# Gate and value products of the first network's last batch by one level of Strassen's method, with the down products laid between them

## The chip, the cores and the metric

One core of a Trainium2 chip runs the whole program. The metric is device time in microseconds (us) from start to end of one execution; lower is better. The engines are named as the profile names them: PE multiplies matrices (PEld is its weight load), DVE works element by element, ACT applies functions and copies, SP issues all DMA transfers of this kernel, in one queue and in order; POOL does almost nothing here. PE writes to eight PSUM banks of 512 fp32 words in each partition, from which DVE or ACT must take the results.

## What is computed

Attention over 4 batches of 512 local tokens (a window of 32 on either side, and 32 global tokens for each batch), then two feed-forward networks on all 4·(512+32) = 2176 rows. The change lies in the first network.

```python
a_l = sm(concat([scale * q_l @ k_g.T, where(|i-j| <= 32, scale * q_l @ k_l.T, -1e9)]))
x = concat([sm(scale * q_g @ k_all.T) @ v_all, a_l @ v_all])   # 2176 rows of 512
# first network: 512 -> 1536 -> 512
g = x @ w_gate;  y = (g * sigmoid(g) * (x @ w_val)) @ w_out
# second network: 512 -> 2048 -> 512
h = y @ w_in;    out = (max(h, 0) + alpha * min(h, 0)) @ w_out2
```

## The kernel before

**Precision.** Each fp32 operand is split into a high and a low part (`hi` by an ACT copy that rounds to fp32r, `lo` by a DVE subtraction). A product is three matmuls, hi·hi, hi·lo and lo·hi (`passes`). The weights arrive as 64-bit floats; `convert` makes them fp32 with two passes of ACT and three of DVE over 1024 words per partition.

**Order of work.** Hidden features come in 12 blocks f of 128, in two halves GA (0 to 5) and GB (6 to 11). Activations lie with features on the partitions and tokens on the columns.

1. Attention of batch 0, then the first network for batches 0, 1 and 2 (512 columns each, two visits of six blocks per batch, `visit1`). In a visit each block has a gate product (12 matmuls of 512 columns into bank `g`, `mm12`), an ACT Silu, a value product (bank `v`), a DVE multiplication and the split of `h`; the down product of the block before (12 matmuls) is added up in banks `acc0` to `acc3`. The attention of the next batch, the conversion of weights, and `w2_prepare` (see below) are laid between the blocks by a `pump`.
2. Batch 3 and the 128 global rows, 640 columns, in four visits: columns 0 to 255 and 256 to 639, each for GB and for GA, with the same products in pieces of 256 or 384 columns (L856 for gate and value, L894 for down). After the second visit of each range the sums lie in `y3` and `yg`.
3. The second network, on three chunks of 768, 768 and 640 columns and eight pairs j of hidden blocks. Its first product already uses Strassen's method in Winograd's form (`up`: seven products of 6 matmuls, L1216, where plain blocks need eight; DVE adds at L1224 and L1254; an ACT copy at L1247), its second is plain (`down`, L1284).

**Weights of the second network.** `w2_prepare` is a generator: for each of 16 matrices it loads 1 MB of 64-bit words, converts it, forms Strassen's four sums (L838), splits, and stores high and low parts in DRAM, from where `fetch` loads them later. The pump takes a step of it when nothing else is to be converted; what is left is taken during batch 3.

**What sets the order.** Everything up to `nc.flush()` (all of step 1) is recorded, and `Planner` lays it out by a list schedule: each operation has a price by its engine and size, PE's order of recording gives target times, and an operation on another engine is due `SLACK` = 60 us after its target, or sooner if PE needs it. Behind the flush, the framework's own scheduler orders the code nearly as written. On each engine instructions are taken in order.

**Room.** Weights of the first network lie in six 1 MB slots for gate and value (`wgv`) and three for down (`wo`). The operands of the matmuls of a batch, high and low, lie in `xa` (4 × 640 columns each).

## Time and profile before

| | |
|---|---|
| three runs | 896.65 us median, 895.0 to 897.09 |
| profiled execution: its time, its span | 896.52 us, 894.7 us |
| PE busy | 875.3 us, 98% of the span |
| PEld, DVE, ACT busy | 761.3, 607.6, 501.2 us |
| granted PE clock, mean | 0.996 |
| moved by DMA | 217.25 MB, 243 GB/s |

The span runs from the first to the last instruction; what lies around it is 1.8 us. A busy engine counts from the start to the modelled end of each instruction. The profile gives shares for the whole program; the stages differ, so the views below are taken by stage.

### The profile page before, as it was taken

What the parts mean: (1) busy time and instruction counts of PE and PEld (TensorE: products, weight loads), DVE (VectorE), ACT (ScalarE), POOL (GpSimd) and SP (SyncE); (2) the same over time, 40 slices, a digit from 0 to 9 for tenths busy, and PEclk for the clock granted to TensorE, in tenths of its full rate; (3) what the DMA queues carried; (4) which work ended last, traced back from release to release, by engine and by line L of the source; (5) the groups of instructions that cost most, each with busy time, mean ns of one, the idle gap of its engine ahead of it and who ended that gap; (6) DMA issues with size and microseconds to landing.
All of it is one profiled execution on the core that took longest, in us unless ns stands there. A gap on an engine that the chain in (4) does not pass through costs nothing.

```text
span 894.7 us, 17087 instructions
## 1 busy us (share of the span) xinstructions
PE 875.3 (98%) x6940; PEld 761.3 (85%) x6940; DVE 607.6 (68%) x1261; ACT 501.2 (56%) x1007; POOL 0.7 (0%) x6
## 2 busy tenths in 40 slices
PE   5899999999999999999999999999999999999997
PEld 4677778788788787889999999999999999989896
DVE  3898889856377465567411257777896777977776
ACT  5889999767586584555312125434555434554442
POOL 0000000000000000000000000000000000000000
PEclk9899999999999999999999999999999999999999
DMA  9799988688957568744463255646375554675631
GB/s 345 267 410 412 363 327 338 263 325 306 375 191 279 224 243 323 282 182 148 167 225 127 95 180 203 228 159 262 145 265 229 209 215 174 250 275 222 279 141 59
DMA packets 34030, 217.25 MB, mean 243 GB/s; under 512 B 4000, under 2 KB 4640, under 8 KB 10272
## 3 DMA queue, kind: packets, MB, share of 16 engines
q1 hardware_dynamic: 33952, 216.17, 63.5%
q8 instruction: 54, 0.88, 0.4%
q14 instruction: 24, 0.20, 0.1%
HBM read 167.66 MB, written 48.50 MB: 242 GB/s over the span
## 4 chain that ended last, share of the span: by engine, by line
PE 60%; DVE 0%; issue 0%
PE ps_acc L1284 21%; PE ps_a L1216 8%; PE ps_v L1216 5%; PE ps_g L1216 5%; PE ps_acc L894 5%; PE ps_v L856 5%; PE ps_g L856 5%; PE acc L270 2%; PE v L270 2%; PE g L270 2%; PE a L270 0%; DVE dbl L270 0%; DVE oacc L1289 0%; DVE h L270 0%
## 5 line engine op out<-in xcount | busy, mean ns | idle before, releaser
L1284 PE MATMUL ps_acc<-w,hring 128*128 128x512 f32 x816 | 194.1, 391 | 0.0
L1284 PEld LDWEIGHTS ps_acc<-w,hring 128*128 128x128 f32 x816 | 152.1, 188 | 29.8
L270 PE MATMUL g<-xa,w 128*128 128x512 f32 x432 | 107.7, 398 | 1.8 <-ACT sg L270 1.0
L270 PE MATMUL v<-xa,w 128*128 128x512 f32 x432 | 107.1, 396 | 0.0
L270 PE MATMUL acc<-h,w 128*128 128x512 f32 x432 | 106.4, 395 | 0.6 <-DVE h L270 0.5
L1233 ACT ACTIVATE r<-c 128x384 f32<-128x384 f32 (+1 forms) x96 | 47.9, 499 | 95.8 <-DVE c L1224 95.8
L270 PEld LDWEIGHTS g<-xa,w 128*128 128x128 f32 x432 | 79.0, 188 | 21.4 <-issue 1.8
L1289 DVE TENSOR_TENSOR oacc<-ps_acc,oacc 128x512 f32<-128x512 f32 x119 | 81.8, 690 | 22.3 <-PE ps_acc L1284 21.1
L270 PEld LDWEIGHTS acc<-h,w 128*128 128x128 f32 x432 | 79.8, 188 | 19.7 <-DVE h L270 1.6
L270 PEld LDWEIGHTS v<-xa,w 128*128 128x128 f32 x432 | 79.3, 188 | 18.3 <-issue 1.4
L1238 ACT ACTIVATE hring<-g 128x384 fp32r<-128x384 f32 (+1 forms) x96 | 48.6, 506 | 54.7 <-DVE g L1235 54.2
L270 ACT ACTIVATE e<-e,mx 128x128 f32<-128x128 f32 (+1 forms) x136 | 57.1, 422 | 17.6 <-DVE mx L270 17.4
L1239 DVE TENSOR_TENSOR hring<-g,hring 128x384 fp32r<-128x384 f32 (+1 forms) x96 | 51.1, 532 | 19.4 <-ACT hring L1238 16.4
L1235 DVE SCALAR_TENSOR_TENSOR g<-g,nal,r 128x384 f32<-128x384 f32 (+1 forms) x96 | 56.7, 590 | 10.2 <-ACT g L1234 9.6
L270 ACT ACT_TABLE_LOAD x40 | 51.3, 1283 | 7.7 <-PE g L270 6.4
L1234 ACT ACTIVATE g<-c 128x384 f32<-128x384 f32 (+1 forms) x96 | 47.9, 499 | 13.4 <-DVE hring L1239 13.4
L1216 PE MATMUL ps_a<-w 128*128 128x384 f32 (+1 forms) x288 | 51.4, 326 | 0.0
L920 DVE TENSOR_TENSOR t<-ps_v,sg 128x384 f32<-128x384 f32 (+1 forms) x18 | 10.8, 601 | 55.4 <-PE ps_v L856 51.9
L1216 PEld LDWEIGHTS ps_a<-w 128*128 128x128 f32 x288 | 47.9, 188 | 0.3 <-DVE c L1224 0.3
L856 PE MATMUL ps_v<-xa,w 128*128 128x256 f32 (+1 forms) x288 | 45.1, 308 | 0.0
L856 PE MATMUL ps_g<-xa,w 128*128 128x256 f32 (+1 forms) x288 | 45.1, 308 | 0.0
L270 DVE TENSOR_TENSOR t<-v,sg 128x512 f32<-128x512 f32 x36 | 24.7, 687 | 30.0 <-ACT sg L270 12.1
(184 smaller groups left out, 1354.6 us busy)
## 6 DMA issues: line engine op xcount, KB each, us to landing
dbl<-in_w_dram SPq DMA_DIRECT2D x28, 1024.0 KB, 6.1
w<-w2sx SPq DMA_DIRECT2D x24, 1024.0 KB, 4.8
w<-w2ss SPq DMA_DIRECT2D x24, 1024.0 KB, 6.3
w<-w2so SPq DMA_DIRECT2D x24, 1024.0 KB, 5.4
v<-in_v_dram SPq DMA_DIRECT2D x15, 1024.0 KB, 9.6
qk<-in_qk_dram SPq DMA_DIRECT2D x14, 688.0 KB, 9.3
w2sx<-dbl SPq DMA_DIRECT2D x8, 1024.0 KB, 6.5
w2ss<-dbl SPq DMA_DIRECT2D x8, 1024.0 KB, 5.0
```

Source lines behind the costliest of these rows:

```text
L270: last[o.eng] = getattr(getattr(self.nc, o.eng), o.op)(*o.args, **o.kw)
L856: nc.tensor.matmul(out=o, lhsT=a, rhs=x, start=(i == 0), stop=(i == 11))
L894: mm = nc.tensor.matmul(out=acc[m][:, 0:n], lhsT=a, rhs=x, start=(first and not second), stop=(f == fs[-1] and j == 2 and (second or not h ...
L920: nc.vector.tensor_tensor(out=t[:, 0:nn], in0=v[:, 0:nn], in1=sg[:, 0:nn], op=ALU.mult)
L1216: nc.tensor.matmul(out=o[:, 0:n], lhsT=left(name, a, k), rhs=x[:, b, k, 0:n], start=(i == 0), stop=(i == 5),)
L1233: nc.scalar.activation(out=rr, in_=u, func=ACTF.Relu)
L1234: nc.scalar.activation(out=g, in_=u, func=ACTF.Relu, scale=-1.0)
L1235: nc.vector.scalar_tensor_tensor(out=g, in0=g, scalar=nal[:, i:i + 1], in1=rr, op0=ALU.mult, op1=ALU.add)
L1238: nc.scalar.activation(out=hi, in_=g, func=ACTF.Copy)
L1239: nc.vector.tensor_tensor(out=lo, in0=g, in1=hi, op=ALU.subtract)
L1284: nc.tensor.matmul(out=o, lhsT=a, rhs=x, start=(i == 0), stop=(i == 5))
L1289: nc.vector.tensor_tensor(out=oacc[tb], in0=o, in1=oacc[tb], op=ALU.add)
```

## The change

Batch 3 and the global rows (640 columns) go through the first network in six pairs j of blocks, f = 2j and 2j+1, and no longer in four visits. For each pair, gate and value are each made by `winograd`, now a function that both networks share: columns in two halves of `N3` = 320, input features in two halves of 256, hidden features in two halves of 128; seven products (`NAMES`) of 6 matmuls of 320 columns. They use two banks, `g` and `v`, in turn (`bank3`), since `a0` and `a1` now hold down sums: the eight accumulators of `down3` are the 640 columns of four output blocks, 384 columns in each of `acc0` to `acc3` and 256 in halves of `a0` and `a1`. The down product of pair j-1 is cut into 16 pieces of 3 matmuls, of which one or two follow each product of pair j from the third on.

Strassen needs four sums of each pair's weights (`w1ss`). `w1_sums` makes them from the split weights while these lie in their slots for batch 1: for each pair, for gate and value, two DVE adds of 512 columns for each block (high plus low), four of 256 in `block_sums`, an ACT copy, a DVE subtraction of 1024, and two stores. In batch 3, `fill` loads 4 MB for each pair (weights and sums, gate and value), the next pair's gate slots as soon as this pair's gate products are through. `third` makes the operands (sums of columns, splits) at the end of batch 2. The global rows are kept whole in `yg`, and split there.

`w2_prepare` has finer steps (`convert_steps`, `split_store`), halves its DVE passes behind the flush (`cuts`), and stores from the buffers it worked in; the pump takes 1.7 of its steps at a time and at most 98 before the flush; the rest follow the products of batch 3, one step after each. The planner's due times are capped at 10 us before the end of PE's work. The code of the second network is the same, but for shared functions and the order of sums in a tile.

```diff
+N3 = 320
+NAMES = ("b11", "t2", "t3", "t1", "b21", "t4", "b22")
...
-            d = target[i] + (0.0 if eng[i] == "tensor" else self.SLACK)
+            d = target[i] if eng[i] == "tensor" else min(target[i] + self.SLACK, at - self.LAST)
...
+    def w1_sums(f):
+
+        j = f // 2
+        for i, z in enumerate("gv"):
+            w = wt[(1, f, z)].bitcast(F32)
+            if f % 2 == 0:
+                sums1[z] = ex.tile([128, 1024], F32, tag="y3%d" % i)
+            s = sums1[z]
+            nc.vector.tensor_tensor(
+                out=s[:, 512 * (f % 2):512 * (f % 2) + 512], in0=w[:, 0], in1=w[:, 1], op=ALU.add
+            )
+            if f % 2 == 0:
+                continue
+            for _ in block_sums(s, s):
+                pass
+            w1ss[j, z] = dram.tile([128, 2, 1024], F32, name="w1ss%d%s" % (j, z))
+            hi = xa.rearrange("p h k c -> p (h k) c")[:, :, S:640]
...
+    def split_store(dst, hi, lo):
+
+        nc.scalar.activation(out=hi, in_=lo, func=ACTF.Copy)
+        for a, b in cuts(lo.shape[1]):
+            yield
+            nc.vector.tensor_tensor(out=lo[:, a:b].bitcast(F32R), in0=lo[:, a:b], in1=hi[:, a:b], op=ALU.subtract)
+        nc.sync.dma_start(out=dst[:, 0], in_=hi.bitcast(F32))
+        nc.sync.dma_start(out=dst[:, 1], in_=lo)
...
-        visit1(1, 0, 512, GB, False, p, after_f=reload(GA, GB))
-        visit1(1, 0, 512, GA, True, p, boundary=lambda: xprep(2))
+        visit1(1, GB, False, p, after_f=summing(reload(GA, GB)))
+        visit1(1, GA, True, p, after_f=summing(lambda f, ps: None), boundary=lambda: xprep(2))
...
-        visit1(3, 0, 256, GB, False, p, third=late)
-        visit1(3, 256, 640, GB, False, p, after_f=reload(GA, GB), third=late)
-        visit1(3, 0, 256, GA, True, p, third=late)
-        for _ in w2gen:
-            pass
...
+            for name in NAMES:
+                o = banks()
+                product(o, name)
+                if name == "b11":
+                    s["p1"] = alp.tile([128, NT], F32, tag="p1", name="p1")
+                    nc.scalar.activation(out=s["p1"][:, 0:n], in_=o[:, 0:n], func=ACTF.Copy)
+                elif name == "t2":
+                    s["u2"] = add("u2", o, s["p1"])
+                elif name == "t3":
+                    s["u3"] = add("u3", o, s["u2"])
+                elif name == "t1":
+                    c22 = add("c", o, s["u3"])
+                    u2 = s["u2"]
+                    nc.vector.tensor_tensor(out=u2[:, 0:n], in0=o[:, 0:n], in1=u2[:, 0:n], op=ALU.add)
+                    use(1, 1, c22[:, 0:n])
...
+                yield
...
-        visit1(3, 256, 640, GA, True, p, after_f=more, boundary=last_ops, third=late)
...
+            def gate(f, q, c):
+                nc.scalar.activation(out=sg[f][:, q], in_=c, func=ACTF.Silu)
+
+            def value(f, q, c):
+                t = work.tile([128, 512], F32, tag="t", name="t")[:, 0:N3]
+                hi, lo = (h[:, f, p, N3 * q:N3 * q + N3] for p in range(2))
+                nc.vector.tensor_tensor(out=t, in0=c, in1=sg[f][:, q], op=ALU.mult)
+                nc.scalar.activation(out=hi, in_=t, func=ACTF.Copy)
+                nc.vector.tensor_tensor(out=lo, in0=t, in1=hi, op=ALU.subtract)
...
+                for _ in winograd(N3, ops1, left, bank3, use):
+                    n += 1
+                    if n > 2:
+                        for _ in range(1 if n % 3 else 2):
+                            next(todo, None)
+                    if j or n > 4:
+                        next(w2gen, None)
+                if z == "g":
+                    again(j, z)
+            for _ in todo:
+                pass
+            again(j, "v")
+            todo = down3(j)
```

Three places show how instructions move. First PE, from the last matmuls of batch 2 on; before, the gate (`ps_g`) and value (`ps_v`) products of three pairs of blocks stand first, 24 matmuls of 256 columns to a bank:

```order
L270 MATMUL acc_126<-h_152,w_145 128x512 x3
L856 MATMUL ps_g<-xa,w_133 128x256 x12
L856 MATMUL ps_g<-xa,w_134 128x256 x12
L856 MATMUL ps_v<-xa,w_133 128x256 x12
L856 MATMUL ps_v<-xa,w_134 128x256 x12
```

and now (`w_137`, `w_138`, `xa`, `hring_4298` hold the operands, `w_133` to `w_136` the weights and sums of pair 0):

```order
L272 MATMUL acc_126<-h_152,w_145 128x512 x3
L1214 MATMUL ps_v<-w_137,w_133 128x320 x6
L1214 MATMUL ps_g<-w_138,w_134 128x320 x6
L1214 MATMUL ps_v<-xa,w_134 128x320 x6
L1214 MATMUL ps_g<-xa,w_134 128x320 x6
L1214 MATMUL ps_v<-xa,w_133 128x320 x6
L1214 MATMUL ps_g<-xa,w_133 128x320 x6
L1214 MATMUL ps_v<-hring_4298,w_134 128x320 x6
```

Seven gate products, then seven value products stand one behind another in two banks; pair 0 has no down pieces between them, and the first such piece (L1271) stands behind the fourteenth.

Second DVE at the same place; before, from the last `h` of batch 2 on (`yp_95` takes batch 2's sums, `raw` and `dbl` are `w2_prepare`):

```order
L270 TENSOR_TENSOR h_152<-t_150,h_152 128x512
L740 TENSOR_SCALAR raw<-raw 128x1024
L270 TENSOR_TENSOR yp_95<-acc_121,yp_95 128x2x256
L270 TENSOR_TENSOR yp_95<-acc_122,yp_95 128x2x256
L270 TENSOR_TENSOR yp_95<-acc_125,yp_95 128x2x256
L270 TENSOR_TENSOR yp_95<-acc_126,yp_95 128x2x256
L741 SCALAR_TENSOR_TENSOR dbl<-dbl 128x1024
L744 SCALAR_TENSOR_TENSOR raw<-raw,dbl 128x1024
```

and now, from the last of these four sums on (four sums of columns into `e_115` and `e_116` stand ahead of them, behind the last `h`):

```order
L272 TENSOR_TENSOR yp_95<-acc_126,yp_95 128x2x256
L272 TENSOR_TENSOR xa<-e_115,xa 128x640
L272 TENSOR_TENSOR xa<-e_116,xa 128x640
L760 TENSOR_SCALAR raw<-raw 128x1024
L769 SCALAR_TENSOR_TENSOR raw<-raw,dbl_112 128x512
L1001 TENSOR_TENSOR hring_4298<-y_166,hring_4298 128x2x256
L1001 TENSOR_TENSOR hring_4298<-yg,hring_4298 128x2x64
L1222 TENSOR_TENSOR u_4333<-ps_g,p_4324 128x320
L769 SCALAR_TENSOR_TENSOR raw<-raw,dbl_112 128x512
L1222 TENSOR_TENSOR u_4342<-ps_v,u_4333 128x320
L760 TENSOR_SCALAR raw<-raw 128x1024
L1222 TENSOR_TENSOR c<-ps_g,u_4342 128x320
```

The adds that empty PE's two banks (L1222) now stand behind the splits of operands and between passes of `w2_prepare` (L760, L769).

Third DVE in batch 1, between a value product's `t` and the next softmax; before:

```order
L270 TENSOR_TENSOR t_150<-v_129,sg_148 128x512
L270 TENSOR_TENSOR dbl_111<-raw_131,dbl_111 128x2x512
L270 TENSOR_TENSOR h_151<-t_150,h_151 128x512
L270 TENSOR_SCALAR o_130<-a_113,rc_128 128x64 x2
```

and now:

```order
L272 TENSOR_TENSOR h_151<-t_150,h_151 128x512
L272 TENSOR_TENSOR y_139<-y_139,xa 128x1024
L272 TENSOR_TENSOR raw_131<-raw_131,dbl_111 128x1024
L272 TENSOR_TENSOR o_130<-a_113,rc_127 128x512
L272 TENSOR_TENSOR y_166<-w_134 128x512
L272 TENSOR_TENSOR y_166<-w_133 128x512
L272 TENSOR_TENSOR y_166<-y_166 128x256 x4
```

The rows with `y_139` and `y_166` are `w1_sums`: they stand among the rows that PE waits for.

## Rows read from the trace of the kernel before

**Rows 1.** The page: busy time of each engine, granted PE clock in 40 slices.

```profile
PE 875.3 (98%) x6940; PEld 761.3 (85%) x6940; DVE 607.6 (68%) x1261; ACT 501.2 (56%) x1007; POOL 0.7 (0%) x6
PEclk9899999999999999999999999999999999999999
```

**Rows 2.** Stretches by stage: busy us of each engine, clock, DMA share, GB/s.

```profile
0.00:172.00 172.00, 157.86 (x2089) 124.39 (x2090) 136.85 (x349) 151.22 (x311) 0.70 (x6) 0.98 0.88 340
172.00:300.00 128.00, 127.50 (x1198) 102.00 (x1197) 80.07 (x184) 88.17 (x164) 0.00 (x0) 1.00 0.77 291
300.00:410.00 110.00, 109.85 (x970) 88.88 (x969) 64.39 (x135) 64.94 (x120) 0.00 (x0) 1.00 0.66 249
410.00:537.00 127.00, 127.00 (x867) 127.00 (x866) 47.80 (x82) 33.68 (x63) 0.00 (x0) 1.00 0.43 157
537.00:895.00 358.00, 353.12 (x1824) 319.07 (x1822) 278.54 (x515) 163.19 (x349) 0.00 (x0) 1.00 0.55 207
```

**Rows 3.** The chain that ended last, through batch 3: start, length, work.

```profile
404.71 5.44 PE acc L270 x24
410.15 2.87 PE ps_g L856 x24
413.02 2.88 PE ps_v L856 x24
...
436.06 2.08 PE ps_g L856 x12
...
530.62 6.24 PE ps_acc L894 x36
536.86 1.04 PE ps_g L1216 x6
```

**Rows 4.** Timeline in the second network's third chunk (320 columns to a product).

```profile
792.16 1.04 PE L1216 MATMUL ps_v<-op,w 128*128 128x320 f32 x6
793.03 1.04 PE L1216 MATMUL ps_g<-op,w 128*128 128x320 f32 x6
793.23 0.44 ACT L1247 ACTIVATE p<-ps_v 128x320 f32<-128x320 f32 x1 [0.64 <-PE ps_v L1216]
793.91 1.92 PE L1216 MATMUL ps_a<-w 128*128 128x320 f32 x12
795.06 0.49 DVE L1224 TENSOR_TENSOR u<-ps_a,u 128x320 f32<-128x320 f32 x1
795.67 2.91 PE L1284 MATMUL ps_acc<-w,hring 128*128 128x512 f32 x12
795.87 0.49 DVE L1224 TENSOR_TENSOR c<-ps_a,u 128x320 f32<-128x320 f32 x1 [0.32 <-PE ps_a L1216]
796.28 0.48 DVE L1254 TENSOR_TENSOR u<-ps_a,u 128x320 f32<-128x320 f32 x1
```

**Rows 5.** Timeline of DVE in batch 1: spacing of passes of 1024, 512 and 256.

```profile
256.95 0.69 DVE L270 TENSOR_TENSOR t<-v,sg 128x512 f32<-128x512 f32 x1 [1.22 <-ACT sg L270]
258.65 1.22 DVE L270 TENSOR_TENSOR dbl<-raw,dbl 128x1024 fp32r<-128x1024 f32 x1 [1.01 <-ACT dbl L270]
259.80 1.22 DVE L270 SCALAR_TENSOR_TENSOR dbl<-dbl 128x1024 int32<-128x1024 int32 x1
260.94 0.68 DVE L270 TENSOR_TENSOR h<-t,h 128x512 fp32r<-128x512 f32 x1
261.54 1.21 DVE L270 SCALAR_TENSOR_TENSOR raw<-raw,dbl 128x1024 int32<-128x1024 int32 x1
275.56 0.43 DVE L270 TENSOR_TENSOR raw<-raw,raw 128x256 f32<-128x256 f32 x1
275.90 0.42 DVE L270 TENSOR_TENSOR raw<-raw 128x256 f32<-128x256 f32 x1
300.40 0.69 DVE L270 TENSOR_TENSOR t<-v,sg 128x512 f32<-128x512 f32 x1 [4.82 <-PE a L270]
```

**Rows 6.** One stretch of four blocks at the end of batch 1, columns as in rows 2.

```profile
256.95:300.40 43.45, 43.45 (x389) 34.56 (x388) 30.63 (x61) 30.03 (x52) 0.00 (x0) 1.00 0.64 235
```

**Rows 7.** Timeline around the end of batch 2.

```profile
404.55 5.60 PE L270 MATMUL acc<-h,w 128*128 128x512 f32 x24
404.86 0.68 DVE L270 TENSOR_TENSOR t<-v,sg 128x512 f32<-128x512 f32 x1
406.46 0.69 DVE L270 TENSOR_TENSOR h<-t,h 128x512 fp32r<-128x512 f32 x1
408.57 2.48 DVE L270 TENSOR_TENSOR yp<-acc,yp 128x512 f32<-128x512 f32 x4
```

**Rows 8.** DMA issues (KB each, median us from issue to landing), and a stretch as in rows 2.

```profile
w<-w2sx SPq DMA_DIRECT2D x24, 1024.0 KB, 4.8
w<-w1s5g SPq DMA_DIRECT2D x2, 1024.0 KB, 9.7
w<-w1s8o SPq DMA_DIRECT2D x1, 1024.0 KB, 11.6
40.00:60.00 20.00, 18.61 (x172) 14.46 (x171) 19.01 (x44) 17.60 (x24) 0.00 (x0) 1.00 1.00 403
```

**Rows 9.** Groups of DVE instructions by shape: busy us, mean ns of one.

```profile
L270 DVE TENSOR_SCALAR raw<-raw 128x1024 f32<-128x1024 f32 x24 | 16.5, 689 | 21.6 <-ACT raw L270 21.6
L1239 DVE TENSOR_TENSOR hring<-g,hring 128x320 fp32r<-128x320 f32 x32 | 15.6, 488 | 6.0 <-ACT hring L1238 4.9
L951 DVE TENSOR_TENSOR yg<-ps_acc,yg 128x128 f32<-128x128 f32 x4 | 1.1, 284 | 0.0
L1007 DVE TENSOR_TENSOR w<-tsum,w 128x768 fp32r<-128x768 f32 x3 | 2.9, 958 | 0.5 <-ACT w L1006 0.5
```

More of the change, by code (lines that the diff above doesn't have):

```diff
@@ new lines, in visit1, with down @@
+    def visit1(b, fs, last, pump, after_f=None, boundary=None):
+        acc = [bank(f"acc{m}") for m in range(4)]
+        hs = {}
+        def down(f):
+            h, w = hs.pop(f), weight((1, f, "o"))
+            with nc.atom():
+                for m in range(4):
+                    wm = [w[:, p, 128 * m:128 * m + 128] for p in range(2)]
+                    for j, (a, x) in enumerate(passes(wm, [h[:, p] for p in range(2)])):
+                        nc.tensor.matmul(
+                            out=acc[m], lhsT=a, rhs=x, start=(f == fs[0] and j == 0), stop=(f == fs[-1] and j == 2),
+                        )
+            if after_f:
+                after_f(f, "o")
+        for i, f in enumerate(fs):
@@ L1127 @@
+        visit1(2, GB, True, p, after_f=before_third, boundary=third)
+        while wq:
+            wload(True)
         assert st["k"] >= mark[4] + 9 and not stores
```

471 lines of the change are left out of this document (252 added, 219 removed).

## Prediction

> **What bounds the kernel now.** I began with the page: PE is busy 875.3 of 894.7 us, and its granted clock is at nine tenths or more in every slice but the second [rows 1]; that is the upper of its two levels, 2.4 GHz. DVE and ACT stand far below. Then I took the stages apart [rows 2]. From 172 us on PE has hardly a gap (127.50 of 128.00, 109.85 of 110.00, 127.00 of 127.00); most of its idle time lies ahead of 172 us, where nothing changes: PE's order is the same there and that of the others nearly so. The chain of waits [rows 3] then shows what PE does in batch 3: gate, value and down products one behind another, each starting when the one before ends, from 410.15 to 536.86 us. So time is saved by taking columns from PE there, and lost wherever another engine lets PE wait. DVE is busy only 47.80 of 127 us in batch 3, but 80.07 of 128 in batch 1 and 64.39 of 110 in batch 2 [rows 2]; those are the rooms into which the change puts work.
>
> **Term 1: PE's products, -10.6 us.** Taken away: for each of 12 blocks, gate and value, 12 matmuls of 256 columns and 12 of 384. Twenty-four of 256 take 2.88 us and twelve of 384 take 2.08 [rows 3], so 12 · 2 · (1.44 + 2.08) = 84.5 us. The down products have 288 matmuls of the same two widths before and after, 12 · 12 · (0.120 + 0.173) = 42.2 us; together 126.7, which is the stretch of batch 3, so it holds no gap. Added: 6 pairs · 2 · 7 products · 6 = 504 matmuls of 320 columns. The second network's third chunk has them: twelve from 793.91 to 795.67 us, 0.1467 each [rows 4]. 504 · 0.1467 = 73.9 us. The difference is 10.6.
>
> **Term 2: pair 0, where DVE can't follow, +4.2 us.** A product of 6 matmuls takes 0.88 us. A bank is read from 0.20 us behind PE's last start (795.67, add at 795.87), an add of 320 columns takes 0.49, and adds that don't wait for each other start 0.41 apart [rows 4]. With two banks in turn, product k+2 needs k's bank when k+1 ends, 0.88 us after k: 0.20 + 0.49 fits, if DVE is free. In pair 0 it isn't. Let T0 be the end of batch 2's last down product. In the row of before `h` ends at 407.15, 3.0 us ahead of T0, and the four `yp` sums begin 1.6 ahead of it [rows 7]. Now one more split of 640 columns stands ahead of `h`, so I let DVE go on from T0 - 2.4. Up to the first add that empties a bank it has, in order: four sums of columns (two of 512, two of 128; 0.60 and 0.28: 1.8 us), the four `yp` (2.4), two splits of 640 (0.73 each, between 0.49 for 320 and 0.96 for 768, less 0.08 by which passes overlap), two pieces of `w2_prepare` (0.6 each), and 0.9 for the last operand [rows 5, 7, 9]: 7.8 us. So the second product's bank comes free at about T0 + 5.8; PE wants it at T0 + 2.6. That first add starts at T0 + 5.4. From its start to the end of the add that frees the bank for the last product but one, the printed order has 11 adds (0.41) and 8 pieces of 512 or 1024 of `w2_prepare` (0.6): 9.3 us without a pause, so T0 + 14.7; two more products (1.76) end at T0 + 16.5. PE alone would need 14 · 0.88 = 12.3. The loss is 4.2 us. Bounds: 1.5 if DVE comes to T0 with its four sums of columns done (then the operand of the third product and the double add of `t1`, 0.20 + 0.41 + 0.48 against 0.88, remain); 7 if a `w2_prepare` pass in this stretch also has to wait for a load or a store, which takes 4.8 us in the median to land [rows 8].
>
> **Term 3: pairs 1 to 5 and the start of the second network, +1.0 us.** Here down pieces lie between the products: a pair takes PE 12.3 + 42.2/6 = 19.3 us, while DVE has 16 adds, 4 multiplications and 4 subtractions, 24 · 0.41 = 9.8 us, and, for pairs 1 and 2, up to 8 us of `w2_prepare`. Between one product's end and the reuse of its bank lie about 1.8 us. So I cost these pairs at nothing but 0.1 us each for the double add, and give 0.5 to the switch: accumulators now lie in `a0` and `a1`, which the second network's third product wants, and must be emptied first (eight small copies). Before, it went on without a gap [rows 3]. Bounds 0 and 3. The gate weights of the next pair, 2 MB, have from the end of the gate products to the next pair, 9.7 us (7 in pair 0); 1 MB lands in 4.8 us in the median [rows 8]. I cost that at nothing; the rival below prices it.
>
> **Term 4: the weight sums in batch 1, +1.5 us.** `w1_sums` adds 24 passes of 512, 48 of 256 and 12 of 1024 to DVE: with spacings of 0.60, 0.34 and 1.15 [rows 5] that is 14.4 + 16.3 + 13.8 = 44.5 us, and 12 copies on ACT. DVE's idle time in batches 1 and 2 together is 47.9 + 45.6 us [rows 2], but `w2_prepare` competes for it. The order piles it up at the end of batch 1: in the four blocks from 256.95 to 300.40 the count of 1024 passes stays at 11, that of 512 goes from 17 to 27 and that of 256 from 4 to 25. DVE was busy 30.63 us there [rows 6]; plus 10 · 0.60 + 21 · 0.34 = 13.1 makes 43.8 in 43.45 us. So it is full, and in order; when it waits for ACT (1.0 and 1.2 us here [rows 5]) it falls behind. PE bears some of that: after a value product it has a down and a gate product, 2 · 2.72 us [rows 3], before it needs the bank `v` again. Lateness up to about 5 us costs nothing; the next is that the value product waits for `t`, and behind it the whole of PE's queue. Bounds 0 and 6; I take 1.5, nearer to no loss, because the overload lasts four blocks. Transfers there rise from 37 to 44 MB by the shapes in the queue, so from 291 to about 345 GB/s, under the 403 that a full stretch shows [rows 2, 8]. The stores of `xa` go in pieces of 512 bytes, for which no row has a price.
>
> **The sum.** 896.5 - 10.6 + 4.2 + 1.0 + 1.5 = 892.6 us, against the profiled execution's own 896.52, which is 0.1 us under the median of the three runs.
>
> A rule speaks against the change. The rows above say that one add fits between two uses of a bank (0.69 of 0.88 us). The Trainium skill, "Perfetto Trace Analysis" (Identifying Performance Opportunities; Matmuls), says that a gap that repeats on the engine that should be full can mean too few PSUM buffers, and that independent groups should rotate through banks; here a rotation of four becomes one of two. By the rows the sum is 892.6; by the rule, with every product paying, it is the last rival below. No run so far has two banks.
>
> **The rivals.**
> *DVE keeps up everywhere.* Terms 2 to 4 at their lower bounds: 896.5 - 10.6 + 1.5 = 887.4 us; with small losses up to 889. For it: DVE is idle for two thirds of batch 3 before. Against it: the printed order of pair 0.
> *DVE late in batch 1 too.* Term 4 at 6 and term 2 at 5: 898.0; the case holds 894 to 899. For it: the full four blocks. Against it: PE's 5 us of patience.
> *Slower: gate weights land late.* One queue in order, 5 MB for each pair instead of 9 MB for all of batch 3; at each of five changes of pair PE waits for the first product's weights. It decides once three transfers need more than 9.7 us; single ones took 9.7 and 11.6 in full stretches [rows 8]. At 12 us: 892.6 + 5 · 2.3 = 904. For it: stores and loads of `w2_prepare` in the same queue, each behind an engine. Against it: 5 MB in 19.3 us is 270 GB/s.
> *Slower: two banks are too few.* If DVE, busy with something else, is 0.3 us late at each of the 84 products, that is 25 us, less what term 2 holds already: 914 or so. For it: an add has 0.19 us to spare in pair 0. Against it: 1.8 us to spare in the others.
>
> **How the numbers follow.** The forecast (889 to 894) has 0.48, DVE keeping up 0.14, DVE late 0.26, late weights 0.08, too few banks 0.04. A measurement of this kernel tells 0.3%, 2.7 us, from no change: faster means under 894.0, slower over 899.3. Faster: 0.48 + 0.14, less 0.03 for the forecast's edge: 0.59. Slower: the last two and a little of the third: 0.13. The rest, 0.28, is no change. The range goes from the first rival's 887.4 to 898.5, which leaves out some 0.05 below and 0.14 above.
>
> **What the profile would show.** Right: PE's products of 320 columns in batch 3 at 0.147 us each and 504 of them; gaps of PE of 3 to 6 us in all in the first 17 us behind the last 512-column down product, ended by DVE adds; hardly a gap in pairs 1 to 5; a span of batch 3 near 121 us. In batch 1, DVE over 90% busy at the end and PE gaps of a microsecond or two, ended by `t`. Wrong: gaps at each change of pair that end with a DMA (third rival), a regular gap ahead of each product (fourth), or PE idle by more than 5 us between 172 and 410 us (second).

## The result: 903.6 us, slower than before by 0.8%

The changed kernel took 903.61 us in the median of 4 runs (901.79 to 904.92), the kernel before 896.82 (895.00 to 897.09): a ratio of 1.0079, interval 1.0056 to 1.0101. The forecast was 892.6. The profiled execution took 903.27 us, span 901.5.

The page after, which answers to [rows 1]:

```profile
PE 869.4 (96%) x6868; PEld 749.9 (83%) x6868; DVE 689.9 (77%) x1445; ACT 525.5 (58%) x1049; POOL 0.7 (0%) x6
PEclk9999999999999999999999999999999999999999
```

PE is busy 5.9 us less, and yet the span grew by 6.8. The stretches of the changed kernel by stage, columns as in [rows 2], say where:

```profile
0.00:172.00 172.00, 156.84 (x2095) 122.08 (x2096) 141.73 (x358) 152.84 (x314) 0.70 (x6) 1.00 0.91 350
172.00:308.00 136.00, 132.69 (x1276) 105.46 (x1275) 111.91 (x245) 99.91 (x178) 0.00 (x0) 1.00 0.91 324
308.00:418.13 110.13, 106.51 (x885) 85.40 (x884) 67.68 (x140) 64.79 (x116) 0.00 (x0) 0.98 0.92 324
418.13:434.62 16.49, 13.79 (x86) 12.33 (x85) 16.11 (x33) 8.59 (x15) 0.00 (x0) 1.00 0.82 261
434.62:543.81 109.19, 106.58 (x710) 105.75 (x709) 73.18 (x157) 35.23 (x73) 0.00 (x0) 0.98 0.85 306
543.81:901.50 357.69, 352.98 (x1826) 318.88 (x1824) 279.31 (x517) 164.10 (x356) 0.00 (x0) 1.00 0.55 207
```

Batch 3 begins at 418.13 us; in [rows 3] it begins at 410.15. Batches 1 and 2, in which PE's products are the same as before, now hold 6.9 us of idle PE (0.65 in [rows 2]), and the DMA engines' share there went from 0.77 and 0.66 to 0.91 and 0.92. Pair 0 (fourth row) takes 16.5 us, the rest of batch 3 (fifth) 109.2, so batch 3 takes 125.7 us, 1.0 less than before.

To compare traces I take the time of the same matmul, counted from the start: number 2081 (170.95 us before) and number 4253, the first of batch 3 (409.99 before). Between the two the changed kernel loses 9.4 us; it is 1.3 ahead at the first of them. Of the 9.4, 6.3 are idle time of PE that the kernel before hasn't; another 1.7, by estimate, go to 3.41 us at half clock (granted clock 0.50 from 329.80 us on).

| part | forecast | measured |
|---|---|---|
| ahead of 172 us | 0 | -1.3 |
| batches 1 and 2 (term 4) | +1.5 (0 to 6) | +9.4 |
| PE's products (term 1) | -10.6 | -10.6 |
| pair 0 (term 2) | +4.2 (1.5 to 7) | 16.5 - 12.3 = +4.2 |
| pairs 1 to 5 and the switch (term 3) | +1.0 (0 to 3) | 109.2 - 103.8 = +5.4 |
| second network | 0 | -0.4 |
| sum, from 896.5 | 892.6 | 903.2 |

(103.8 is what 420 products of 0.1467 and 42.2 us of down products take without a gap.)

Pair 0 and the start of pair 1 in the timeline of PE:

```profile
418.13 1.04 PE L1214 MATMUL ps_v<-w,w 128*128 128x320 f32 x6
419.01 1.04 PE L1214 MATMUL ps_g<-w,w 128*128 128x320 f32 x6
421.22 1.14 PE L1214 MATMUL ps_v<-xa,w 128*128 128x320 f32 x6 [1.17 <-ACT p L1230]
423.31 1.14 PE L1214 MATMUL ps_g<-xa,w 128*128 128x320 f32 x6 [0.95 <-DVE u L1222]
...
434.73 1.04 PE L1214 MATMUL ps_v<-w,w 128*128 128x320 f32 x6
435.62 0.28 PE L1271 MATMUL ps_a<-hring,w 128*128 128x256 f32 x1
437.94 1.12 PE L1214 MATMUL ps_g<-w,w 128*128 128x320 f32 x6 [2.05 <-DMA w<-w1ss1g]
438.90 1.69 PE L1214 MATMUL ps_v<-xa,w 128*128 128x320 f32 x6
```

The third product waits for the first bank, which ACT's copy empties, the fourth for the second bank and DVE's add. At pair 1 PE waits 2.05 us for the weight sums, which were issued at 429.39; then six matmuls take 1.69 us instead of 1.04, for the clock is at its lower level:

```profile
439.02:442.43 3.41, 3.41 (x14) 3.41 (x13) 3.03 (x8) 0.47 (x1) 0.00 (x0) 0.50 1.04 420
```

What holds ACT in pair 0 is seen in its timeline; the two L1000 rows split pair 0's last operand, which PE needs only for its seventh product, and stand ahead of the copy `p` (L1230):

```profile
417.55 1.35 ACT L272 ACTIVATE xa<-e 128x640 fp32r<-128x640 f32 x2
420.02 0.63 ACT L1000 ACTIVATE hring<-y 128x512 fp32r<-128x512 f32 x1 [1.12 <-DVE xa L272]
420.55 0.29 ACT L1000 ACTIVATE hring<-yg 128x128 fp32r<-128x128 f32 x1
420.75 0.42 ACT L1230 ACTIVATE p<-ps_v 128x320 f32<-128x320 f32 x1
```

In batch 2 the largest single loss is at 322 to 333 us. The timeline of all engines there:

```profile
324.40 1.13 ACT L272 ACTIVATE raw<-dbl 128x1024 f32<-128x1024 f32 x1 [5.22 <-DMA w2sx<-raw]
...
328.75 0.36 ACT L272 ACTIVATE y<-a 128x256 f32<-128x256 f32 x1
...
329.17 1.50 PE L272 MATMUL a<-qk 64*32 64x128 f32 x62 [1.94 <-ACT y L272]
```

ACT wants to fill `raw` for `w2_prepare` and waits 5.2 us for a store that reads `raw` (issued at 311.71) to land. The copy `y`, behind it in ACT's order, comes late, and PE waits for that. The gap of 1.68 us later in batch 2 is of the same kind; ACT's `sg` stands behind such a wait of 3.4 us:

```profile
392.84 1.12 ACT L272 ACTIVATE raw<-dbl 128x1024 f32<-128x1024 f32 x1 [3.42 <-DMA w2ss<-raw]
395.41 0.58 ACT L272 ACTIVATE sg<-g 128x512 f32<-128x512 f32 x1
396.04 3.06 PE L272 MATMUL g<-xa,w 128*128 128x512 f32 x12 [1.68 <-ACT sg L272]
```

The waits of DVE and of ACT that ended with a transfer, from 172 to 418 us (total, times, longest), first DVE's:

```profile
DVE raw L272 <- DMA w2so<-raw: 8.9, 3, 6.6
DVE y L272 <- DMA w1ss5g<-y: 5.2, 1, 5.2
DVE y L272 <- DMA w1ss3v<-y: 4.5, 1, 4.5
DVE y L272 <- DMA w1ss3g<-y: 2.5, 1, 2.5
DVE y L272 <- DMA w1ss4g<-y: 2.5, 1, 2.5
...
ACT raw L272 <- DMA w2sx<-raw: 11.4, 3, 5.9
```

So passes wait for stores of the buffers that they fill again: `y` holds the weight sums, `raw` the second network's weights. In the kernel before no pass of DVE waited for a transfer there. ACT did, for 24.5 us in all (16.3 for loads, 8.2 for stores), but never for more than 3.8 us at a time, and PE was idle for 0.6 us: the sum of such waits says little, and what stands behind the long ones decides.

### The profile page after: what moved, and what is told of

Same layout as the page of the kernel before. It is cut to its first block, busy times and chain, and to the rows that moved or that the text cites. A ratio compares the mean times of both kernels' runs of the same rounds, so it can differ in the third digit from the quotient of the medians.

```text
span 901.5 us, 17366 instructions
## 1 busy us (share of the span) xinstructions
PE 869.4 (96%) x6868; PEld 749.9 (83%) x6868; DVE 689.9 (77%) x1445; ACT 525.5 (58%) x1049; POOL 0.7 (0%) x6
## 4 chain that ended last, share of the span: by engine, by line
PE 53%; DMA 8%; DVE 6%; ACT 1%; issue 1%; SPq 0%; DVEq 0%; ACTq 0%
PE ps_acc L1422 21%; PE ps_v L1214 9%; PE ps_g L1214 8%; PE ps_a L1214 8%; DMA w2ss<-dbl 3%; PE ps_acc L1271 3%; DMA dbl<-in_w_dram 2%; PE ps_a L1271 2%; DVE y L272 2%; DVE raw L272 1%; DMA w2ss<-raw 1%; DMA w<-w1ss1g 1%; PE acc L272 1%; PE v L272 1%; DMA w2so<-raw 1%
## 5 line engine op out<-in xcount | busy, mean ns | idle before, releaser
L272 PEld LDWEIGHTS g<-xa,w 128*128 128x128 f32 x432 | 78.9, 188 | 24.5 <-ACT sg L272 4.8
L1388 DVE SCALAR_TENSOR_TENSOR g<-g,nal,r 128x384 f32<-128x384 f32 (+1 forms) x96 | 56.7, 591 | 10.3 <-ACT g L1387 9.7
L1214 PE MATMUL ps_v<-xa,w 128*128 128x320 f32 (+1 forms) x288 | 53.8, 322 | 2.0 <-ACT p L1230 1.7
L1214 PE MATMUL ps_g<-xa,w 128*128 128x320 f32 (+1 forms) x288 | 53.5, 319 | 1.3 <-DVE u L1222 0.9
L1214 PEld LDWEIGHTS ps_v<-xa,w 128*128 128x128 f32 x288 | 47.2, 190 | 3.9 <-ACT p L1230 2.3
L1214 PEld LDWEIGHTS ps_g<-xa,w 128*128 128x128 f32 x288 | 47.4, 189 | 2.8 <-DVE u L1222 1.2
```

Of the source, the lines that this page charges most:

```text
L272: last[o.eng] = getattr(getattr(self.nc, o.eng), o.op)(*o.args, **o.kw)
L1214: nc.tensor.matmul(out=o[:, 0:n], lhsT=left(name, a, k), rhs=x[name][:, b, k, 0:n], start=(i == 0), stop=(i == 5),)
L1388: nc.vector.scalar_tensor_tensor(out=g, in0=g, scalar=nal[:, i:i + 1], in1=rr, op0=ALU.mult, op1=ALU.add)
```

## The experiments

The table has all runs, each with the kernel before measured beside it (895.1 to 895.7 us; 896.8 for the change): median, ratio with interval, the loss from matmul 2081 to 4253, pair 0's 84 matmuls and the rest of batch 3. Kernels whose names are followed by * compute with other numbers, as their expectations say.

| kernel | us | ratio | lost, 172 to batch 3 | pair 0 | rest |
|---|---|---|---|---|---|
| the change | 903.61 | 1.0079 (1.0056 to 1.0101) | 9.4 | 16.5 | 109.2 |
| a_no_sums* | 895.02 | 0.9994 (0.9980 to 1.0009) | 0.9 | 20.4 | 104.9 |
| b_sums_no_store* | 894.12 | 0.9985 (0.9974 to 0.9995) | 1.4 | 18.2 | 105.4 |
| m_before_stores | 896.17 | 1.0010 (0.9995 to 1.0025) | 0.8 | - | - |
| g_sums_tiny* | 900.06 | 1.0051 (1.0031 to 1.0070) | 3.1 | 20.9 | 108.9 |
| e_sums_4k* | 905.32 | 1.0119 (1.0101 to 1.0136) | 11.3 | 20.3 | 105.1 |
| h_sums_fp32 | 896.58 | 1.0008 (0.9992 to 1.0024) | 3.7 | 17.1 | 104.4 |
| q_sums_static* | 904.29 | 1.0098 (1.0082 to 1.0115) | 7.5 | 21.2 | 109.1 |
| r_w2_static* | 908.10 | 1.0145 (1.0132 to 1.0158) | 16.4 | 20.5 | 104.6 |
| u_rate_340 | 907.41 | 1.0137 (1.0123 to 1.0150) | - | 23.4 | 108.1 |
| d_w2_less | 904.27 | 1.0095 (1.0081 to 1.0110) | 7.9 | 21.1 | 105.6 |
| y_hold_w2 | 937.53 | 1.0477 (1.0459 to 1.0494) | 11.8 | 14.6 | 144.1 |
| c_pair0_no_w2 | 900.63 | 1.0068 (1.0053 to 1.0083) | 9.0 | 17.4 | 107.0 |
| i_pair0_later | 900.86 | 1.0062 (1.0047 to 1.0077) | 10.2 | 15.9 | 107.6 |
| n_banks8 | 898.78 | 1.0044 (1.0027 to 1.0060) | 9.1 | 12.3 | 108.1 |
| o_both_banks8 | 896.68 | 1.0012 (0.9995 to 1.0029) | 4.6 | 12.4 | 112.8 |
| p_both_banks8_w2 | 897.31 | 1.0020 (1.0003 to 1.0038) | 6.6 | 12.7 | 110.3 |
| w_fp32_banks8 | 896.09 | 1.0012 (1.0000 to 1.0025) | 8.7 | 12.3 | 109.7 |
| x_best | 891.88 | 0.9958 (0.9941 to 0.9976) | 5.0 | 12.3 | 108.5 |

One profile's loss scatters: `h`, `o` and `w` have the same order of instructions up to batch 3 and lost 3.7, 4.6 and 8.7; the change, `c`, `i` and `n`, alike up to batch 3 too, lost 9.0 to 10.2. Verdicts rest on the medians; the profiles tell where, and a profiled execution can lie 4 us beside its kernel's median (`q` 908.7, `c` 904.4, `o` 900.5, `b` 891.4). In `a`, `d`, `m` and `r` a few matmuls of batch 3 stand ahead of the last ones of batch 2, which shifts their last three columns a little. Each edit ahead of the flush (`a`, `b`, `d`, `e`, `g`, `h`, `m`, `q`, `r`, `u`) also makes the planner lay out another order: in `b` and `q` DVE's order agrees with the change's up to 179.6 us and ACT's up to 185.2, and not behind.

### Do the weight sums carry the loss ahead of batch 3?

```diff
-        visit1(1, GB, False, p, after_f=summing(reload(GA, GB)))
+        visit1(1, GB, False, p, after_f=reload(GA, GB))
...
```

> The weight sums are left out: no adds, no splits, no stores of them; where the change loads sums, this loads stored gate and value weights of the same size, so the products are of the same cost but of other numbers. The change lost 9.5 us of PE's time between 172 us and the start of batch 3 (batch 3 began at 418.1 instead of 410.15 us, though PE was 1.3 us ahead at 172). Theory S (the sums carry it, by DVE's time and the queue's): batch 3 starts at 408.5 to 411 us and the run takes 894 to 896.5 us. Rival P (the re-cut passes of w2_prepare carry it, whose first pass on ACT waits for a load or a store): batch 3 still starts after 415 us and the run takes 900 us or more.

Without the sums 0.9 us are lost there, and the run takes 895.0: the sums, with the order that the planner makes for them, carry it. The next kernel keeps their passes and drops their stores:

```diff
-                w1ss[j, z].rearrange("p h (k c) -> p h k c", c=128), hi, s.rearrange("p (k c) -> p k c", c=128)
+                None, hi, s.rearrange("p (k c) -> p k c", c=128)
...
+        if dst is None:
+            return
...
```

> The weight sums are made on DVE and ACT, but not stored (24 stores of 0.5 MB gone); the loads read stored gate and value weights of the same size instead, so the output has other numbers. If DVE's time in batch 1 carries the 9.5 us lost ahead of batch 3, the run stays at 901 to 904 us and batch 3 starts at 416 us or later. If the queue carries it (DMA engines were 0.92 busy in batch 2, 0.63 before), the run takes 895 to 898 us and batch 3 starts near 411 us. Half and half: 898 to 901.

It is as fast as without sums. Its stretch of batch 1 (that of the change stands above):

```profile
172.00:308.00 136.00, 135.88 (x1354) 108.79 (x1353) 124.53 (x276) 107.13 (x191) 0.00 (x0) 1.00 0.78 282
```

DVE is busy 124.5 of 136 us here, more than the 111.9 of the change, and PE 135.9. So DVE's work by itself costs PE nothing here; the loss comes with the stores. Do their bytes alone carry it?

```diff
+                    for z in "gv":
+                        extra = dram.tile([128, 1024], F32, name="extra%d%s" % (f, z))
+                        nc.sync.dma_start(out=extra, in_=yp[0][:, 0].rearrange("p m c -> p (m c)"))
...
```

> The kernel before, with 24 extra stores of 0.5 MB in batch 1 (two behind each block's value product, of a finished output of batch 0 in rows of 4096 bytes, into memory that nobody reads) and nothing else: the bytes of the weight sums' stores alone, without their passes on DVE and ACT and without any product changed. Theory Q (12.6 MB more in a queue that is full in many stretches): batch 3 starts 4 to 9 us later than in the kernel before, run 899 to 904 us. Rival (the queue was 0.7 busy and takes the bytes; the loss of the change comes from its own order of work): under 2.5 us later, run 895 to 898 us.

They don't: 896.2 us, 0.8 lost. Part of `w2_prepare` moved into batch 3, whose queue had room (12 of its loads from 172 us to batch 3, 3 in it, instead of 14 and 1). A full queue alone doesn't stop PE either: for 78 us the DMA engines' share was 1.01, and PE had no gap.

```profile
172.00:250.00 78.00, 78.00 (x783) 62.81 (x782) 33.02 (x101) 45.73 (x94) 0.00 (x0) 1.00 1.01 405
```

These stores read a buffer that nobody fills again. The same stores as in the change at a sixteenth of their bytes (`g`), and with the small pieces gone (`e`):

```diff
+        r = slice(0, 8 if alt else 128)
-        nc.sync.dma_start(out=dst[:, 0], in_=hi.bitcast(F32))
+        nc.sync.dma_start(out=dst[r, 0], in_=hi[r].bitcast(F32))
...
```

> All 24 stores of weight sums stand where they stood, with their waits for DVE and ACT, but each stores 8 of 128 partitions (0.8 MB in all instead of 12.6); the loads of sums read stored weights of the same size, so the output has other numbers. Theory Q (the bytes of the stores fill the queue's engines): 1 to 2.5 us lost between 172 us and batch 3, run 893.5 to 897 us, as without stores (894.1). Rival O (the queue is issued in order, and a store that waits for DVE holds up the loads behind it): 6 us or more lost, run 900 us or more.

```diff
-        nc.sync.dma_start(out=dst[:, 0], in_=hi.bitcast(F32))
+        nc.sync.dma_start(out=dst[:, 0], in_=lo if alt else hi.bitcast(F32))
...
```

> The high half of each weight sum is not stored from its place in xa (pieces of 512 bytes); in its stead the contiguous low half is stored twice (pieces of 4096 bytes). As many stores, as many bytes, the same passes; the loaded high halves are other numbers. By the pieces' times of the change's trace (512 bytes 28 ns, 4096 bytes 173 ns) the 12 stores of 6.3 MB take 16.6 us of 16 engines instead of 21.5. If the small pieces carry the loss ahead of batch 3 (9.0 and 9.4 us between 172 us and its start in two kernels with these stores, 1.4 without): 3 to 5 us lost there, run 898 to 900.5 us. If the bytes carry it: still 6.5 to 9 us lost, run 901.5 to 904 us.

`g` lost 3.1 us ahead of batch 3, nearer to no stores than to full ones, but its run, 900.1, lies between. `e` lost no less than the change, so the loss doesn't need the 512-byte pieces (both of its stores read `y`, though, and DVE waits up to 6.2 us for one). Half of the bytes for pairs 1 to 5, with their splits moved into batch 3, in a version that computes all:

```diff
+            if j:
+                nc.sync.dma_start(out=w1ss[j, z], in_=s)
+                continue
...
+                    s = flat3(z)
+                    nc.scalar.activation(out=flat[:, 0:1024], in_=s, func=ACTF.Copy)
+                    nc.vector.tensor_tensor(out=flat[:, 1024:2048], in0=s, in1=flat[:, 0:1024], op=ALU.subtract)
+                    land3(j + 1, z)
```

> The sums of pairs 1 to 5 are stored once, as fp32 in rows of 4096 bytes (0.5 MB instead of 1 MB for each of 10), land in batch 3 a pair ahead in a free buffer and are split there: 10 copies of 1024 on ACT and 10 subtractions of 1024 on DVE move from batch 1 to batch 3. All is computed. By theory Q 5.2 MB fewer are stored in batches 1 and 2 and none in small pieces but pair 0's: 3 to 5 us lost ahead of batch 3 instead of 9.2; the 2.05 us wait for sums at pair 1 is gone with the slow clock behind it. Run 895.5 to 899 us. Rival (the splits hold up DVE and ACT in batch 3, 1.15 us each time): what is won ahead of batch 3 is lost again in it, run 901 us or more.

896.6 us, as expected: 7 us less than the change. The wait for sums at pair 1 is gone, and the rest of batch 3 falls to 104.4.

### Which wait is it?

```diff
+        fixed = yp[0][:, 0].rearrange("p m c -> p (m c)")
-        nc.sync.dma_start(out=dst[:, 1], in_=lo)
+        nc.sync.dma_start(out=dst[:, 1], in_=fixed.rearrange("p (k c) -> p k c", c=128) if alt else lo)
...
```

> All passes of the weight sums and all 24 stores of 0.5 MB stay, but the stores read a finished output of batch 0 (rows of 4096 bytes) instead of the buffers that the passes use again; so no pass waits for a store of sums to land. The loaded sums are other numbers. Theory W (DVE and ACT, in order, wait for these stores: 15.3 us of DVE's waits in the change's trace ended with one): 2 to 4.5 us lost between 172 us and batch 3 instead of 9.0 to 10.2, run 896.5 to 899.5 us. Rival V (w2_prepare's buffers carry it, 8.9 us of DVE and 17 us of ACT): 7 us or more lost, run 901 us or more.

The windows of `q`, batch 1 and batch 2:

```profile
172.00:308.00 136.00, 136.00 (x1330) 108.58 (x1329) 116.64 (x250) 98.80 (x177) 0.00 (x0) 1.00 0.86 333
308.00:418.00 110.00, 103.63 (x863) 83.36 (x843) 67.17 (x136) 65.91 (x117) 0.00 (x0) 0.98 0.91 318
```

With all stores but no wait for them PE has no gap in batch 1. But batch 2 loses more than in the change, 6.4 us of idle PE, and the run takes 904.3. So theory W holds for batch 1 and not for the run. Both long gaps of batch 2 stand behind a wait of ACT for a store that reads `raw`:

```profile
359.40 1.12 ACT L272 ACTIVATE raw<-dbl 128x1024 f32<-128x1024 f32 x1 [5.26 <-DMA w2sx<-raw]
367.20 0.66 PE L272 MATMUL a<-ident,o 128*128 128x128 f32 x4 [2.89 <-ACT pt L272]
392.73 1.12 ACT L272 ACTIVATE raw<-dbl 128x1024 f32<-128x1024 f32 x1 [4.26 <-DMA w2ss<-raw]
395.33 4.27 PE L272 MATMUL g<-xa,w 128*128 128x512 f32 x12 [2.97 <-ACT sg L272]
```

ACT's waits for stores of `raw` add up to 20.7 us in `q`, 17.0 in the change and 10.3 in `b`, where none is longer than 2.8.

```diff
-        nc.sync.dma_start(out=dst[:, 1], in_=lo)
+        nc.sync.dma_start(out=dst[:, 1], in_=lo if alt else yp[0][:, 0].rearrange("p m c -> p (m c)"))
...
```

> The weight sums are as in the change; the low halves of w2_prepare, which it makes in place in its two raw buffers and stores from there, are made in place still, but the stores of these 0.5 MB read the finished output of batch 0; so nobody waits for a raw buffer's store. The second network's weights are other numbers. Theory V: 2 to 5 us lost ahead of batch 3, and less loss at the change from pair 0 to 1; run 895 to 899 us. Theory W: 7 us or more lost, run 900.5 us or more. Both in part: 5 to 7 us lost.

Both theories missed: 908.1, 16.4 lost. ACT's passes no longer wait for the raw buffers' stores but for loads (18.4 us of waits for `dbl`). One wait taken away brought another. It doesn't show what waits for stores of `raw` cost, since these loads come in their place.

```diff
-    TABLE, DMA, START, LAST = 1.28, 405.0, 0.75, 10.0
+    TABLE, DMA, START, LAST = 1.28, 340.0, 0.75, 10.0
```

> Only the planner's rate for the queue changes, from 405 to 340 GB/s (full stretches of the change moved 342 to 358); the program's work and buffers are the same, the order of batches 0 to 2 is another. All is computed. Theory R (passes are placed by the planner ahead of transfers that land later than it assumes, and block DVE and ACT): 3 to 6 us lost ahead of batch 3, run 896.5 to 900.5 us. If no order avoids the waits: 8 us or more lost, run 902 us or more.

907.4 us. Batch 3 begins at 415.25, 2.9 earlier than in the change, but pair 0 takes 23.4 and the rest 108.1. (PE's order differs, so no loss from 172 us is given.)

```diff
-    pr_xp=0, pr_acc=0, pr_lda=0, wage=3, w2n=1.7, w2max=98, cp0=0.5, cp1=0.0,
+    pr_xp=0, pr_acc=0, pr_lda=0, wage=3, w2n=1.4, w2max=82, cp0=0.5, cp1=0.0,
```

> w2_prepare advances more slowly ahead of batch 3 (1.4 steps a slot instead of 1.7, at most 82 instead of 98 steps), and the rest goes between the products of batch 3; all is computed. If the crowding of ACT, DVE and the queue in batch 2 carries the 5.8 us lost there, 2 to 4 us of them come back, batch 3 has 16 steps more and loses 0 to 1: run 900 to 902 us. If batch 1 carries all and batch 2 only hands it on, or the steps block batch 3: 903 to 906 us.

No gain. The steps that the planner no longer holds are, in part, moved forward again by the scheduler: in `p_both_banks8_w2`, which has the same numbers, the first pass of a later step stands at 353.9 us, though the code writes it behind products that begin at 415.6:

```profile
L757 ACT ACTIVATE raw<-dbl x5: 1114/1119/1126, 353.9 to 431.4; 128x1024 f32<-128x1024 f32 x5
```

To hold them, their loads were queued behind batch 3's weight loads:

```diff
-                    if j or n > 4:
-                        next(w2gen, None)
+                    if j:
+                        with tc.issue_after(held[0].ins):
+                            for _ in range(2):
+                                next(w2gen, None)
...
```

> The change with its weight sums and all their stores, but with fewer steps of w2_prepare ahead of batch 3 (at most 64 of 128) and the loads of the rest queued behind batch 3's own weight loads, so that the scheduler can't move them forward into batch 2 (in c_pair0_no_w2, d_w2_less and p_both_banks8_w2 it did); two steps follow each product of pairs 1 to 5. All is computed. Theory F (a queue that is 0.88 to 0.93 busy between 172 us and batch 3 makes loads land late wherever the bytes come from; at 0.83 or less 0 to 3 us are lost): the share falls to 0.77 to 0.83 and 0 to 3.5 us are lost there, though the sums' passes, stores and buffers are all as they were. The 33 us of DVE passes that move into batch 3 then lengthen it: the run itself may take 896 to 905 us. Rival (the sums' stores cost what they cost, whatever else is in the queue): 7 us or more lost ahead of batch 3.

```profile
172.00:423.24 251.24, 242.44 (x2177) 193.70 (x2176) 156.40 (x353) 152.06 (x281) 0.00 (x0) 0.99 0.73 260
423.24:581.97 158.73, 131.97 (x794) 125.35 (x793) 116.08 (x238) 60.63 (x102) 0.00 (x0) 0.92 0.90 330
308.00:327.00 19.00, 19.00 (x265) 14.93 (x263) 10.24 (x31) 10.94 (x28) 0.00 (x0) 1.00 1.04 333
340.00:423.24 83.24, 83.24 (x613) 68.00 (x612) 24.58 (x50) 33.13 (x62) 0.00 (x0) 1.00 0.43 152
```

Theory F's numbers fail: at a share of 0.73 over the stretch, as in the kernel before, 11.8 us are lost, 8.3 of them at one place near 327 us where ACT waits 4.7 us for `raw`'s store and PE 5.2 for `y` behind it. But the mean hides the place. What was taken away stood behind it (the orders of ACT, DVE and the queue are the change's up to 328 us); in the 19 us ahead of this loss the queue was as full as in the change (third row, 1.04; 1.06 there from 308 to 324.4 us), and where the share fell, to 0.43, PE has no gap (fourth row). So the run doesn't speak against a full queue as one of the causes; it speaks against the mean share as a measure. Batch 3 grew by 33 us: PE waits there for weights' loads (5.7 us at the longest) and for the values' copies on ACT (7.7 us in all).

### Pair 0

```diff
-                    if j or n > 4:
+                    if j:
```

> The steps of w2_prepare are kept out of pair 0 (they begin with pair 1); all is computed. Theory D (DVE's other work delays the emptying of the two banks): the 14 products of pair 0 took 16.5 us from the last 512-column down product, against 12.3 of PE alone; now 13.5 to 15. The wait of 2.05 us for the sums' load at the head of pair 1, and the 3.4 us at half clock behind it (1.7 us lost), vanish or halve, since a 0.5 MB store and a 1 MB load leave the queue. Run 898 to 901 us. Rival L (the load is late by itself): pair 0 shorter, the wait at pair 1 as long as pair 0 became shorter, run 902 to 904.

```diff
-        x_split(2, ops1["b22"], (1, 1))
...
+                    if j == 0 and n == 2:
+                        x_split(2, ops1["b22"], (1, 1))
```

> Pair 0 without w2_prepare's steps, and the split of its last operand (b22) behind its second product instead of ahead of the first. All is computed. ACT's copy that empties the first bank waited behind that split (PE idle 1.2 us and more), DVE's add for the second bank behind it and the other splits (0.9 us). If these queues are the cause of pair 0's 16.5 to 17.4 us: 13.5 to 15 us now, and the clock stays at its upper level there; run 898.5 to 901 us. If the wait only moves to another operand (xa's splits): 16 us or more, run 901 to 903.5 us.

(`i` has the line of `c` too.) They take 900.6 and 900.9 us, some 3 less than the change, but pair 0 takes 17.4 and 15.9: DVE and ACT have the operands' splits there in any case. In `c` the first two gaps are as long as in the change (1.17 and 0.94 us), yet behind them the clock is at its lower level:

```profile
425.70 1.97 PE L1214 MATMUL ps_g<-xa,w 128*128 128x320 f32 x6 [0.94 <-DVE u L1222]
425.73:429.14 3.41, 3.41 (x13) 3.41 (x14) 2.59 (x6) 3.41 (x4) 0.00 (x0) 0.50 0.42 168
```

That is 1.7 us by estimate; without it pair 0 would be 0.8 shorter than in the change. The wait for sums at pair 1 is shorter (1.46 and 0.64 us instead of 2.05), and batch 3 takes 124.4 and 123.5 us instead of 125.7.

```diff
+            if turn["i"] <= 14:
+                return bank(("v", "g", "a0", "a1", "acc0", "acc1", "acc2", "acc3")[turn["i"] % 8 - 1])
...
```

> Only pair 0 changes: its 14 products go through all eight banks in turn (the accumulators of the down products are not in use before pair 1) instead of two. All is computed. Theory B (PE waits in pair 0 because two banks wait for DVE and ACT, which are behind): pair 0 takes 12.4 to 14 us instead of 16.5 to 17.4, no half clock behind a gap there; run 898.5 to 900.5 us. Rival (operands that are split late, b22 above all): pair 0 15 us or more, run 902 us or more.

```profile
418.79:431.10 12.31, 12.31 (x85) 12.31 (x84) 11.94 (x24) 7.12 (x13) 0.00 (x0) 1.00 0.90 334
```

With eight banks pair 0 has no gap while DVE is as busy as before: 12.31 us, and the run takes 898.8. So two banks are what makes the backlog of ACT and DVE PE's.

How much that costs varies from kernel to kernel. In `a`, `b`, `d`, `e`, `g`, `q`, `r` and `u` pair 0 is written as in the change and takes 18.2 to 23.4 us: the third product waits 2.0 to 7.6 us for ACT's copy, and the clock falls to 0.50 in pair 0 in each of them. In `a`, without any stores of sums:

```profile
416.64 1.19 PE L1214 MATMUL ps_v<-xa,w 128*128 128x320 f32 x6 [3.17 <-ACT p L1230]
418.60 1.97 PE L1214 MATMUL ps_g<-xa,w 128*128 128x320 f32 x6 [0.77 <-DVE u L1222]
```

### Together

> Sums of pairs 1 to 5 stored once as fp32 and split in batch 3 (as in h_sums_fp32), pair 0 without steps of w2_prepare and with the last operand's split later (as in i_pair0_later), and eight banks in pair 0. All is computed. If the three causes add up: 3 to 4.5 us lost ahead of batch 3, pair 0 12.4 to 13.5 us, pairs 1 to 5 104.5 to 105.5 us; run 889.5 to 893 us, faster than the kernel before. If what pair 0 no longer waits for comes back in pair 1 (DVE is only put off): 894 to 897 us.

> As o_both_banks8, with fewer steps of w2_prepare ahead of batch 3 (1.4 a slot and at most 82) and more between the products of batch 3, where the queue has been relieved of 5 MB. All is computed. If bytes ahead of batch 3 carry the loss there: 1.5 to 3 us lost instead of 3.7, run 888 to 891 us. If the steps hold up DVE in batch 3: its pairs 1 to 5 take over 106 us, run 892 to 895 us.

> Sums of pairs 1 to 5 stored once as fp32 (as in h_sums_fp32) and eight banks in pair 0 (as in n_banks8), without the later steps of i_pair0_later. All is computed. If o_both_banks8 lost the gain of the banks because it moved the steps of w2_prepare and the landing of the sums into pair 1 (3.0 us of PE's waits there, 1.7 at half clock): batch 3 takes 117.5 to 119.5 us, 3.7 us lost ahead of it, run 890.5 to 894 us. If pair 1 always pays for what pair 0 no longer waits for: batch 3 121 us or more, run 895 to 897.5 us.

All three take 896 to 897 us, no better than `h` alone: the gains don't add up. In `o` pair 0 ends early and PE then waits for the values' copies, by which the first down products are late (timeline of PE); the clock is at 0.50 for 6.8 us behind that:

```profile
433.01 0.50 PE L1284 MATMUL ps_a<-hring,w 128*128 128x256 f32 x2 [2.73 <-ACT hring L1339]
```

The last kernel is `w` with at most 96 steps of `w2_prepare` ahead of batch 3 and the loads of the rest held as in `y`, one step a product:

> Sums of pairs 1 to 5 stored once as fp32, eight banks in pair 0, at most 96 steps of w2_prepare ahead of batch 3 and the loads of the rest queued behind batch 3's weight loads. All is computed. Theory F: share of the queue between 172 us and batch 3 0.83 to 0.86 instead of 0.89, 1 to 3 us lost there, batch 3 118 to 121 us; run 889 to 893 us, faster than the kernel before. If the 11 us of DVE passes that come into batch 3 hold up its products: batch 3 123 us or more, run 894 to 898 us.

```profile
172.00:413.73 241.73, 237.85 (x2159) 191.17 (x2158) 162.60 (x359) 153.95 (x284) 0.00 (x0) 0.99 0.80 291
413.73:426.04 12.31, 12.31 (x85) 12.30 (x84) 10.70 (x22) 4.67 (x10) 0.00 (x0) 1.00 0.76 260
426.04:534.51 108.47, 106.16 (x710) 104.29 (x709) 92.77 (x188) 50.49 (x89) 0.00 (x0) 1.00 0.86 303
```

891.9 us, 0.42% under the kernel before and 11.7 us under the change. Batch 3 takes 120.8 us, 5.9 less than before; 5.0 are still lost ahead of it, more than the 1 to 3 expected. 3.3 of them are one gap, and it stands behind a pass of sums that waits for a store of its buffer, with DVE at work without a pause between:

```profile
255.15 1.29 DVE L272 TENSOR_TENSOR y<-w 128x512 f32<-128x512 f32 x2 [4.73 <-DMA w1ss0v<-y]
265.88 1.16 PE L272 MATMUL a<-qk 64*32 64x128 f32 x64 [3.33 <-DVE o L272]
```

## Why the prediction was wrong

**Term 1 held.** Where nothing waits, 84 products take 12.31 us, 0.1466 each.

**Term 2 held, with another first waiter, and its exactness is luck.** The 14 products ended at T0 + 16.5, as worked out. The first gap waits for ACT's copy rather than for a DVE add; the term has ACT in no place, and in eight kernels with the same pair 0 the copy came so late that pair 0 took 18.2 to 23.4 us. The loss of 4.2 us is gone with eight banks instead of two. The Trainium skill, "Perfetto Trace Analysis" (Optimizing Tensor Performance; Matmuls), wants independent groups to rotate through banks; pair 0 agrees. My reading of it, that every product pays, doesn't hold: from pair 1 on a wait for a bank is rare (one, 0.56 us). Nor did the change take banks away from these products: before, they had `g` and `v` alone too, and the rotation of four is the second network's.

**Term 4 failed, and it is the step that made the forecast wrong.** It had +1.5 us, at most 6; measured are +9.4. "DVE is full, and in order" was right at the end of batch 1 (busy 43.2 of 44 us from 264 to 308 us), but no gap of PE there ended with `t`, and in `b` the same work beside PE left it 0.1 us idle in all of batch 1. What was mis-sized is the sentence on transfers: I compared a mean of 345 GB/s with the 403 of a full stretch and took the queue for free. Without the 24 stores the run is 9.5 us shorter (894.1 against 903.6), and 8.0 us of the difference lie between 172 us and batch 3 (1.4 lost against 9.4, in profiles that lie 11.8 us apart). The stores read buffers that the next pass fills; 15.3 us of DVE's waits end with them, and `w2_prepare`'s stores from `raw` land later beside them (by group 9.5, 10.0 and 7.6 us in the median against 6.7, 7.7 and 7.1 in `b`), so that ACT waits too. What stands behind such a pass in ACT's or DVE's order then stops PE. The sign that I had named for the second rival, PE idle by more than 5 us between 172 and 410 us, came true (6.9), but not by a full DVE.

**Term 3 failed at one place.** The late-weights rival came true once, at pair 1, instead of at each of five changes: 2.2 us of wait, and 1.6 more for twelve matmuls at half clock, which I hadn't priced. A wait for ACT that ends at 479.66 costs 0.7. Some 0.9 is spread. The rival's 904 is near the result by chance: most of the loss lies ahead of batch 3.

**Still open.** Both parts are needed, as far as these runs go: the stores without the passes (`m`, on the kernel before) cost 0.8 us, the passes without the stores (`b`) 1.4. The longest gaps of PE ahead of batch 3 in the change, `q`, `y` and `x` all stand behind a wait of 3.4 to 5.3 us of ACT or DVE for a store of the buffer that it fills again, with the queue's share at 0.88 to 1.05 in that time; that a full queue makes such a store land late is argued from these places and not shown by a run of its own. `r`, which took away some of these waits, lost as much and more through loads. And since the planner lays out another order for each of `a`, `b`, `e`, `g`, `h`, `q` and `r`, none of them shows how much of a loss belongs to the stores and how much to the order of passes that comes with them. `u` alone changed the order on purpose, and its run was 3.8 us longer than the change's.
